# A gated mix of a 2D spectral filter and a state-space recurrence on one core: the last recurrence units moved ahead of the last output tiles, and the start reordered

## The chip, the cores and the metric

The kernel runs on one core of one Trainium2 chip. The core has five engines, each with its own instruction stream taken in order: PE multiplies matrices (its weight loads are listed apart as PEld), DVE, ACT and POOL work elementwise, SP only issues transfers (DMAs), which ACT and POOL can issue too. PE writes its products into PSUM, from which ACT or DVE copies them to SBUF, the working memory. The metric is the device time of one execution in microseconds (us), the median of several.

## What is computed

The input x has 2048 rows (time) of 1024 features. Branch A filters x in the frequency plane, branch B runs a complex linear recurrence with 1024 states over time, and a gate per row mixes the two.

```python
X = rfft2(x); a = irfft2(X * (w_r + 1j * w_i)).astype(bfloat16)        # branch A
Lam_bar = exp(exp(log_dt) * Lam); Bu = einsum("bld,pd->blp", x, B_bar)  # branch B
for t in range(L): h = Lam_bar * h + Bu[:, t]
y = 2 * einsum("blp,dp->bld", hseq, Cmat).real + x * Dskip
g = sigmoid((x * gate_w).sum(-1, keepdims=True))
return g * a + (1 - g) * y
```

## The kernel before

Transforms and the products of branch B are matrix products on PE. The order of PE, DVE and ACT is written out by hand: within these three engines the instructions stand in the order in which the Python code emits them. SP and POOL are ordered by the framework's own scheduler. The work runs in these stages:

- **Fronts.** x arrives in eight loads of 512 KB (`load_x`, L192). `turn_x(j)` (L625) transposes one of 16 row groups on PE and copies it to `xQ` on ACT; `fold(j)` (L631) makes `preT` of it on DVE. A front j (L730) turns two row groups, folds one, takes one step of the transform along the features (`ps_fd` L330 on PE, `X` L333 on ACT) and one of the transform along time (`ps_s` L344 to L347 on PE, `A` L349 on DVE for j under 7, else on ACT), and stores `A` to DRAM. From j = 8 each front also has half a recurrence unit and pieces of the rotation tables (`make_tab`, L203: DVE makes the angle `ang`, ACT `rot_kk`, `sn_f`, `cs_f` and the scaled copies `t`, DVE the table `tab`). After fronts 9, 11, 13 and 15 `gate` (L656) makes four columns of the gate; its result `zsb` goes through DRAM on POOL's queue (L664, L666) and comes back as `zt`.
- **Recurrence units.** `unit(c, q)` (L247) is a chunk c of 256 rows and a half q of the states. PE makes the two halves `psu` (L295, 32 products each), ACT copies each to `h` (L297), and DVE then has seven pieces of work: two rotations back (L256, L257), a join (L262 to L265), two scans (L269), the carry (L275 to L277), two rotations forth (L281, L282) and a join (L287, L288). The pieces wait in a Python list; `vector(us)` (L306) emits as many as an assumed budget allows, and `vector_until(c)` all that chunk c needs.
- **Spectral middle.** After the fronts, "w", "z", "q" and "qn" correct one column (through DRAM and back as `Bcol`, L357 and L360, on POOL's queue, and with `gate_end`, L668, which makes `omg`, `gB` and `grat` from `zt`). Then 16 groups are multiplied by the filter (L445 to L482) and 8 turned back (L487 to L501), each interleaved with a half unit or half of an `early` tile.
- **Output tiles** of 128 rows. The first ten are `early(tb)` (L566): branch B alone is finished, scaled by `omg` and parked in DRAM as `ye`. `late_tile(i)` (L605) closes one later: `spectral` (L582: eight products `ps_id` L588, a copy L591 on ACT, four additions L593 to L597 on DVE), plus the parked tile (L607 on DVE), then the store. The last six, `own_tile(tb)` (L610), hold both branches in one PSUM tile: 16 products L557 and five small ones per half (L561 with `dgD`, the diagonal of the skip weights; L564 adds the spectral part `ga`), a copy L618 on ACT, the store. `own` (L857) makes `ga` of the next tile between the two halves.

The last stage runs from the end of chunk 6's first unit: `unit(6, 1)`, own tile 10, `unit(7, 0)`, own tile 11, `unit(7, 1)`, then own tiles 12 to 15 with the ten late tiles beside them; the counts in the table of L868 say how many late tiles follow each half.

Of the kernel before, what the change touches and what calls it, by code (L numbers as in the profile page):

```python
# [13 lines left out]
FP32 = mybir.dt.float32  # L14
# [91 lines left out]
def kernel(  # L106
# [215 lines left out]
    def gfnet():  # L322
# [16 lines left out]
        for j in range(16):  # L339
            X1 = X1_next  # L340
            if j + 1 < 16:
                X1_next = fd(j + 1)
            psa = psA.tile([P, 2, K], FP32, name="ps_s1", tag="ps")
            nc.tensor.matmul(psa[:, 0, :], lhsT=T3_sb[:, j, 0, :], rhs=X1[:, 0, :], start=True, stop=False)  # L344
            nc.tensor.matmul(psa[:, 0, :], lhsT=T3_sb[:, j, 1, :], rhs=X1[:, 1, :], start=False, stop=True)
            nc.tensor.matmul(psa[:, 1, :], lhsT=T3_sb[:, j, 0, :], rhs=X1[:, 1, :], start=True, stop=False)
            nc.tensor.matmul(psa[:, 1, :], lhsT=T3_sb[:, j, 2, :], rhs=X1[:, 0, :], start=False, stop=True)  # L347
            A1 = gta.tile([P, 2, K], BF16, name="A1", bufs=3)
            (nc.vector.tensor_copy if j < 7 else nc.scalar.copy)(out=A1, in_=psa)  # L349
            if j:  # L350
                nc.vector.tensor_copy(out=Acol[:, j - 1, :], in_=A1s[j - 1][:, :, 0])
            A1s[j] = A1
            nc.sync.dma_start(out=turn1_dram[j].rearrange("r m k -> m r k"), in_=A1)
            yield "s1"
# [148 lines left out]
    def after_ia():  # L503
        ictx.close()
        hpool[1] = ctx.enter_context(tc.tile_pool(name="hpB", bufs=NHB, side="right", reuse_waits="tile"))
        lp = ctx.enter_context(tc.tile_pool(name="lp", bufs=1, side="right", reuse_waits="tile"))
        fft["lp"] = lp
        load_xs(0)
        fft["dgD"] = lp.tile([P, 8, P], BF16, name="dgD")
        for d8 in range(8):  # L510
            nc.vector.tensor_scalar_mul(out=fft["dgD"][:, d8, :], in0=ident, scalar1=dskT[:, d8:d8 + 1])
        fft["gt"] = bctx.enter_context(tc.tile_pool(name="gt", bufs=3, side="right", reuse_waits="tile"))
        fft["wp"] = bctx.enter_context(tc.tile_pool(name="wp", bufs=1, side="right", reuse_waits="tile"))
        fft["Sel"] = fft["gt"].tile([P, 4, P], BF16, name="Sel_sb", tag="gc1", bufs=2)
        nc.sync.dma_start(out=fft["Sel"], in_=cKRS.rearrange("p (i m) -> p i m", m=P)[:, 2:6])
        fft["Wb"] = [fft["wp"].tile([P, 2, 2, K], BF16, name=f"Wb{i}") for i in range(3)]
        for w in fft["Wb"]:
            nc.gpsimd.memset(w[:, 0, :, 0:1], 1.0)
            nc.gpsimd.memset(w[:, 1, :, 0:1], 0.0)
# [111 lines left out]
    def fold(j):  # L631
        preTs[j] = gta.tile([P, 8, P], BF16, name="preT", bufs=4)
        nc.vector.tensor_add(out=preTs[j][:, 0:4], in0=xQ[:, 0:4, j, :], in1=xQ[:, 4:8, j, :])
        nc.vector.tensor_sub(out=preTs[j][:, 4:8], in0=xQ[:, 0:4, j, :], in1=xQ[:, 4:8, j, :])

    load_x(0)
    nc.sync.dma_start(out=fft["G"], in_=cG)
    load_x(1)
    load_T3(0, 4)
    for i in range(2, 5):  # L640
# [5 lines left out]
    for j in range(2):  # L646
        turn_x(j)
        fold(j)

    turn_x(2)  # L650
    fold(2)
    assert step() == "fd"
    zsb = cpool.tile([P, 16], FP32, name="zsb")
    zt = cpool.tile([P, 16], FP32, name="zt")

    def gate(r0, n):  # L656
        zps = psX.tile([P, n], FP32, name="zps_g", tag="pt")
        for r in range(r0, r0 + n):
            for d8 in range(8):
                nc.tensor.matmul(zps[:, r - r0:r - r0 + 1], lhsT=xQ[:, d8, r, :], rhs=gwT[:, d8:d8 + 1],  # L660
                                 start=(d8 == 0), stop=(d8 == 7))
        nc.vector.tensor_copy(out=zsb[:, r0:r0 + n], in_=zps)
        if r0 + n == 16:
            nc.gpsimd.dma_start(out=z_dram, in_=zsb)  # L664
            with nc.allow_non_contiguous_dma(reason="gate by token tiles"):
                nc.gpsimd.dma_start(out=zt, in_=z_dram.rearrange("(t a) j -> (a j) t", a=8))  # L666
# [63 lines left out]
    def front(pieces=0):  # L730
        j = at[0]
        at[0] += 1
        for r in (2 * j + 3, 2 * j + 4):
            if r < 16:
                turn_x(r)
        if 3 <= j + 2 < 16:
            fold(j + 2)
        assert step() == "s1"
        for load, *args in order.get(j, ()):
            load(*args)  # L740
        for _ in range(pieces):
            next(tables, None)
# [65 lines left out]
    tables = chain(*(make_tab(jp) for jp in range(4)))  # L808
    while at[0] < 16:
        j = at[0]  # L810
        front(0 if j < 4 else 1 if j < 6 else 2 if j < 9 else 3)
        if j >= 8:
            halves(ssm, 1)
        if j >= 9:
# [13 lines left out]
    for v, n in (("w", 3), ("z", 2), ("q", 2), ("qn", 1), ("s2", 0), ("uv", 1)):  # L828
        assert step() == v
        if v == "z":  # L830
            gate_end()
        for _ in range(n):
            halves(ssm, 1)
            vector(3.0)
    for g in range(16):
        assert step() == "is1"
        assert step() == "uv"
# [23 lines left out]
            yield v  # L861

    ga[NEARLY] = spectral(NEARLY, grat, own_home(NEARLY))
    for _ in chain(unit(6, 1), own(10), unit(7, 0), own(11), unit(7, 1)):
        vector(4.0)
    for i in range(4):
        yl[i] = late_load(i)
    for tb, counts in ((12, (0, 2)), (13, (1, 1)), (14, (2, 2)), (15, (2, 0))):  # L868
        for _, n in zip(own(tb), counts):
            vector(4.0)  # L870
            for _ in range(n):
# [35 lines left out]
```

## Time and profile before

| what | us |
|---|---|
| median of 3 runs (lowest to highest) | 371.21 (369.28 to 371.55) |
| the profiled execution's own time | 370.46 |
| span, from its first to its last instruction | 367.9 |
| PE busy, 92% of the span | 338.0 |
| DVE busy, 81% | 298.1 |
| ACT busy, 48% | 177.1 |
| transfers: 62.17 MB, mean 169 GB/s | |

Numbers of the trace are us from the span's start. A row of the timeline has the start, the busy time, the engine, the line in the code, the operation, what is written and read, the count of merged instructions, and in brackets how long the engine was idle before and what released it. PE's products overlap, so 32 products of 273 ns each pass in about 3.5 us; distances between starts are the safer measure. The profile's clock row shows what the throttle granted (0.989 on average).

### The profile page before, as it was taken

What the parts mean: (1) busy time and instruction counts of PE and PEld (TensorE: products, weight loads), DVE (VectorE), ACT (ScalarE), POOL (GpSimd) and SP (SyncE); (2) the same over time, 40 slices, a digit from 0 to 9 for tenths busy, and PEclk for the clock granted to TensorE, in tenths of its full rate; (3) what the DMA queues carried; (4) which work ended last, traced back from release to release, by engine and by line L of the source; (5) the groups of instructions that cost most, each with busy time, mean ns of one, the idle gap of its engine ahead of it and who ended that gap; (6) DMA issues with size and microseconds to landing.
All of it is one profiled execution on the core that took longest, in us unless ns stands there. A gap on an engine that the chain in (4) does not pass through costs nothing.

```text
span 367.9 us, 6395 instructions
## 1 busy us (share of the span) xinstructions
PE 338.0 (92%) x2488; PEld 226.6 (62%) x2521; DVE 298.1 (81%) x483; ACT 177.1 (48%) x216; POOL 21.0 (6%) x54
## 2 busy tenths in 40 slices
PE   2899899599999999999999999999999999999980
PEld 1455367376876665666656576795957667565540
DVE  1168855889779999999999999929368699999596
ACT  3499987465431265555656325453432223253620
POOL 7310111100030000000000000000000000000000
PEclk9999999999999999999999999999999999999995
DMA  7999999975582148899997367551202262025863
GB/s 225 331 316 202 208 232 205 208 204 132 182 208 22 67 132 199 237 252 274 265 275 199 108 177 206 141 172 57 87 12 76 57 228 59 2 57 163 238 228 115
DMA packets 83310, 62.17 MB, mean 169 GB/s; under 512 B 54320, under 2 KB 71248, under 8 KB 83024
## 3 DMA queue, kind: packets, MB, share of 16 engines
q1 hardware_dynamic: 82688, 61.70, 62.4%
q0 software_dynamic: 512, 0.05, 1.1%
q8 instruction: 19, 0.31, 0.4%
q14 instruction: 11, 0.09, 0.1%
q10 hardware_dynamic: 80, 0.01, 0.0%
HBM read 31.32 MB, written 17.84 MB: 134 GB/s over the span
## 4 chain that ended last, share of the span: by engine, by line
PE 65%; DVE 17%; DMA 9%; issue 4%; ACT 4%; SPq 0%; ACTq 0%; DVEq 0%
PE ps_y L557 22%; PE psu L295 21%; PE ps_fd L330 4%; PE ps_is L497 4%; DVE h L269 3%; DMA turn_scratch<-A 3%; DMA CT<-in_A_x_dram 2%; PE ps_id L588 2%; PE ps_is L472 2%; PE ps_is L473 2%; PE ps_s L448 2%; PE ps_y L561 2%; DMA out_dram<-raw 1%; DMA raw<-turn_scratch 1%; DMA turn_scratch<-C 1%
## 5 line engine op out<-in xcount | busy, mean ns | idle before, releaser
L295 PE MATMUL psu<-xQ,BT 128*128 128x256 bf16 x1024 | 116.1, 273 | 3.9 <-ACT h L297 3.3
L557 PE MATMUL ps_y<-CT,h 128*128 128x512 bf16 x493 | 113.5, 379 | 0.9
L295 PEld LDWEIGHTS <-BT 128*128 128x128 bf16 x1024 | 100.1, 98 | 19.9 <-issue 4.9
L557 PEld LDWEIGHTS <-h 128*128 128x128 bf16 x512 | 50.3, 99 | 55.0
L269 DVE TENSOR_TENSOR_SCAN h<-rz,h 128x1024 bf16<-128x1024 f32 x32 | 72.3, 2281 | 0.3
L297 ACT CAST h<-psu 128x1024 bf16<-128x1024 f32 x32 | 32.3, 1010 | 59.9 <-PE psu L295 59.9
L330 PE MATMUL ps_fd<-G_sb,preT 128*128 128x512 bf16 x118 | 30.9, 396 | 4.0 <-ACT X L333 1.8
L256 DVE TENSOR_TENSOR su<-h,tab 128x2048 bf16<-128x2048 bf16 x16 | 19.6, 1222 | 17.8 <-ACT h L297 17.3
L575 ACT ACTIVATE ye<-ps_y,omg 128x512 f32<-128x512 f32 x20 | 12.7, 683 | 36.6 <-PE ps_y L561 25.2
L333 ACT CAST X<-ps_fd 128x1024 bf16<-128x1024 f32 x16 | 20.9, 1307 | 7.4 <-PE ps_fd L330 6.6
L330 PEld LDWEIGHTS <-preT 128*128 128x128 bf16 x128 | 12.3, 100 | 17.4 <-issue 4.4
L499 ACT CAST ZT<-ps_is 128x1024 bf16<-128x1024 f32 x16 | 15.4, 1020 | 10.7 <-PE ps_is L497 10.7
L257 DVE TENSOR_TENSOR h<-h,tab 128x2048 bf16<-128x2048 bf16 x16 | 19.6, 1225 | 1.0
L282 DVE TENSOR_TENSOR h<-h,tab 128x2048 bf16<-128x2048 bf16 x16 | 19.6, 1225 | 0.5
L281 DVE TENSOR_TENSOR sg<-h,tab 128x2048 bf16<-128x2048 bf16 x16 | 19.5, 1219 | 0.1
L450 ACT CAST X<-ps_s 128x1024 bf16<-128x1024 f32 x16 | 16.2, 1014 | 6.8 <-PE ps_s L448 6.8
L628 PE MATMUL pt<-ident,CT 128*128 128x128 bf16 x128 | 10.3, 240 | 8.5 <-DMA CT<-in_A_x_dram 8.5
L629 ACT COPY xQ<-pt 128x1024 bf16<-128x1024 bf16 x16 | 15.5, 1016 | 5.4 <-PE pt L628 5.4
L475 ACT CAST C<-ps_is 128x1024 bf16<-128x1024 f32 x16 | 16.1, 1007 | 2.9 <-PE ps_is L473 2.8
L588 PE MATMUL ps_id<-raw,ZT 128*128 128x256 bf16 x128 | 15.8, 273 | 0.4 <-ACT raw L591 0.4
L591 ACT ACTIVATE raw<-ps_id,grat 128x1024 bf16<-128x1024 f32 x6 | 6.7, 1114 | 18.3 <-PE ps_id L588 18.3
L497 PE MATMUL ps_is<-KRS_sb,raw 128*128 128x128 bf16 x128 | 15.3, 311 | 0.2 <-DMA raw<-turn_scratch 0.2
(182 smaller groups left out, 386.9 us busy)
## 6 DMA issues: line engine op xcount, KB each, us to landing
y_scratch<-ye SPq DMA_DIRECT2D x20, 256.0 KB, 3.9
BT<-y_scratch SPq DMA_DIRECT2D x10, 512.0 KB, 5.0
CT<-in_A_x_dram SPq DMA_DIRECT2D x8, 512.0 KB, 10.3
turn_scratch<-A SPq DMA_DIRECT2D x16, 256.0 KB, 3.1
Bb<-turn_scratch SPq DMA_DIRECT2D x16, 256.0 KB, 4.7
turn_scratch<-C SPq DMA_DIRECT2D x16, 256.0 KB, 3.9
raw<-turn_scratch SPq DMA_DIRECT2D x16, 256.0 KB, 4.4
Wb<-in_A_w_r_dram SPq DMA_DIRECT2D x32, 127.8 KB, 3.7
```

Of the source, the lines that this page charges most:

```text
L256: nc.vector.tensor_mul(out=su, in0=u[:, ::-1], in1=bc(1))
L257: nc.vector.tensor_mul(out=u, in0=u, in1=bc(0))
L269: nc.vector.tensor_tensor_scan(out=seg, data0=rz[:, js].rearrange("p j t -> p (j t)"), data1=seg, initial=0.0, op0=ALU.mult, op1=ALU.add)
L281: nc.vector.tensor_mul(out=sg, in0=u[:, ::-1], in1=bc(3))
L282: nc.vector.tensor_mul(out=u, in0=u, in1=bc(2))
L295: nc.tensor.matmul(psu[:, j, :], lhsT=BT[4 * q + j][:, ri, d8, :], rhs=xQ[:, d8, :, 16 * c:16 * (c + 1)], start=(d8 == 0), stop=(d8 == 7))
L297: nc.scalar.copy(out=u[:, ri].rearrange("p b (q j) -> p b q j", j=16), in_=psu.rearrange("p b (j q) -> p b q j", j=16))
L330: nc.tensor.matmul(ps[:, cls, :], lhsT=preTs[j][:, 4 * cls + d4, :], rhs=G_sb[:, cls, d4, :], start=(d4 == 0), stop=(d4 == 3))
L333: nc.scalar.copy(out=X1.rearrange("p r (i c) -> p c r i", c=2), in_=ps.rearrange("p c (r i) -> p c r i", r=2))
L497: nc.tensor.matmul(pv[:, :, g::4], lhsT=Cq[:, g, P * kc:P * (kc + 1)], rhs=KRS_sb[:, 1, :], start=True, stop=True)
L557: nc.tensor.matmul(psy[:, 512 * dh:512 * (dh + 1)], lhsT=hs[c, jb // 4][:, ri, jb % 4, P * tq:P * (tq + 1)], rhs=CT[ri][:, jb, 512 * dh:51 ...
L588: nc.tensor.matmul(pse[:, slot, :], lhsT=ZT_t[:, i, tb, :], rhs=fft["Gi"][:, i, :], start=(kb == 0), stop=(kb == 1))
```

## The change

Six edits, in the order of the program:

- **Start.** Eight throwaway products (zeros times zeros, into a PSUM tile that nothing reads) stand on PE ahead of everything, four more after the first two row groups are turned. The table `G` is loaded in two halves. The first feature transform stands ahead of the third row group's turn.
- **Folds** are made one front earlier: `fold(j + 3)` in front j.
- **Copies.** `A` is copied by DVE up to j = 9 instead of 6; `zsb` by ACT instead of DVE. Front 9 emits two table pieces instead of three.
- **`dgD`** (eight small scalings on DVE) leaves the spot right after the fronts and is emitted between two pieces of unit (1, 0) in stage "w".
- **POOL's queue**: not in the diff, but its four small transfers come out in another order.
- **End.** Units (6, 1), (7, 0) and (7, 1) come one after another ahead of own tile 10; the late tiles follow the halves of own tiles 11 to 14 one by one, the last two the first half of own tile 15.

```diff
-            (nc.vector.tensor_copy if j < 7 else nc.scalar.copy)(out=A1, in_=psa)
+            (nc.vector.tensor_copy if j < 10 else nc.scalar.copy)(out=A1, in_=psa)
...
-        for d8 in range(8):
-            nc.vector.tensor_scalar_mul(out=fft["dgD"][:, d8, :], in0=ident, scalar1=dskT[:, d8:d8 + 1])
...
+    idle = gta.tile([P, K], BF16, name="idle", tag="A1", bufs=3)
+    nc.vector.memset(idle, 0.0)
+
+    def keep_warm(n):
+        psw = psA.tile([P, 2, K], FP32, name="psw", tag="ps")
+        for i in range(n):
+            nc.tensor.matmul(psw[:, i % 2, :], lhsT=idle[:, 0:P], rhs=idle, start=True, stop=True)
+
+    keep_warm(8)
     load_x(0)
-    nc.sync.dma_start(out=fft["G"], in_=cG)
+    for cls in range(2):
+        nc.sync.dma_start(out=fft["G"][:, cls], in_=cG[:, cls])
...
     for j in range(2):
         turn_x(j)
         fold(j)
-
+    keep_warm(4)
+
+    assert step() == "fd"
     turn_x(2)
     fold(2)
-    assert step() == "fd"
...
-        nc.vector.tensor_copy(out=zsb[:, r0:r0 + n], in_=zps)
+        nc.scalar.copy(out=zsb[:, r0:r0 + n], in_=zps)
...
-        if 3 <= j + 2 < 16:
-            fold(j + 2)
+        if 3 <= j + 3 < 16:
+            fold(j + 3)
...
-        front(0 if j < 4 else 1 if j < 6 else 2 if j < 9 else 3)
+        front(0 if j < 4 else 1 if j < 6 else 2 if j < 10 else 3)
...
-        for _ in range(n):
+        for i in range(n):
             halves(ssm, 1)
             vector(3.0)
+            if v == "w" and i == 1:
+                for d8 in range(8):
+                    nc.vector.tensor_scalar_mul(out=fft["dgD"][:, d8, :], in0=ident, scalar1=dskT[:, d8:d8 + 1])
...
-    for _ in chain(unit(6, 1), own(10), unit(7, 0), own(11), unit(7, 1)):
+    for _ in chain(unit(6, 1), unit(7, 0), unit(7, 1)):
         vector(4.0)
     for i in range(4):
         yl[i] = late_load(i)
-    for tb, counts in ((12, (0, 2)), (13, (1, 1)), (14, (2, 2)), (15, (2, 0))):
+    for tb, counts in ((10, (0, 0)), (11, (1, 1)), (12, (1, 1)), (13, (1, 1)), (14, (1, 1)), (15, (2, 0))):
```

What the edits do to the engines' order shows at three places. The first is ACT in fronts 10 to 12, before: the copies `X` (L333) and `A` (L349) of a front, the table work (`rot_kk`, `sn_f`, `cs_f`, `t`), and `h` (L297), which empties the only PSUM tile that the recurrence units have in this stage.

```order
L333 CAST X_848<-ps_fd 128x2x512
L349 CAST A_855<-ps_s_850 128x1024
L224 ACTIVATE t_759<-cs_f,ci 128x256 x2
L771 ACTIVATE rot_kk<-ang 128x512
L772 ACTIVATE sn_f<-ang 128x512
L297 CAST h<-psu 128x1024
L333 CAST X_931<-ps_fd 128x2x512
```

The same engine after, from the same front 10 on (lines past L633 have moved by some nine: L780 is L771, L781 is L772, L783 is L774):

```order
L333 CAST X_862<-ps_fd 128x2x512
L349 CAST A_869<-ps_s_864 128x1024
L783 ACTIVATE cs_f<-rot_kk,chpi 128x512
L219 ACTIVATE t_878<-sn_f,ci 128x256 x2
L224 ACTIVATE t_879<-cs_f,ci 128x256 x2
L297 CAST h<-psu 128x1024
L333 CAST X_949<-ps_fd 128x2x512
```

Before, `rot_kk` of the fourth table, which needs DVE's `ang`, stands between front 10's `A` and the copy `h`; after, the third table's rest stands there, and the fourth `rot_kk` comes a front later, behind front 11's `A`.

The second place is the end of POOL's queue, after its last presets of a filter tile: the small transfers of the gate (`zsb` out, `zt` back) and of the one column (`Acol` out, `Bcol` back). Before:

```order
L518 MEMSET Wb_1403 128x2
L519 MEMSET Wb_1403 128x2
L664 DMA z_scratch<-zsb 128x16
L357 DMA col_scratch<-Acol 128x32
L666 DMA zt<-z_scratch 128x16x1
L360 DMA Bcol<-col_scratch 128x16x2
```

After (L673 is L664, L675 is L666):

```order
L516 MEMSET Wb_1412 128x2
L517 MEMSET Wb_1412 128x2
L357 DMA col_scratch<-Acol 128x32
L360 DMA Bcol<-col_scratch 128x16x2
L673 DMA z_scratch<-zsb 128x16
L675 DMA zt<-z_scratch 128x16x1
```

The gate's way out and back stood around the column's; it now stands wholly behind it.

The third place is ACT at the end, which copies for PE and so shows PE's order: `h` is a unit, `raw` (L591) the spectral part of an own tile, `BT` (L591) that of a late tile, L618 the close of an own tile. Before, from the spectral part of own tile 10 on:

```order
L591 ACTIVATE raw<-ps_id,grat 128x1024
L297 CAST h<-psu 128x1024 x2
L591 ACTIVATE raw<-ps_id,grat 128x1024
L618 ACTIVATE raw<-ps_y,omg 128x1024
L297 CAST h<-psu 128x1024 x2
L591 ACTIVATE raw<-ps_id,grat 128x1024
L618 ACTIVATE raw<-ps_y,omg 128x1024
L297 CAST h<-psu 128x1024 x2
L591 ACTIVATE raw<-ps_id,grat 128x1024
L618 ACTIVATE raw<-ps_y,omg 128x1024
L591 ACTIVATE BT_131<-ps_id,gB 128x1024
L591 ACTIVATE BT_132<-ps_id,gB 128x1024
```

After, from the same place (L589 is L591, L616 is L618):

```order
L589 ACTIVATE raw<-ps_id,grat 128x1024
L297 CAST h<-psu 128x1024 x6
L589 ACTIVATE raw<-ps_id,grat 128x1024
L616 ACTIVATE raw<-ps_y,omg 128x1024
L589 ACTIVATE raw<-ps_id,grat 128x1024
L589 ACTIVATE BT_131<-ps_id,gB 128x1024
L616 ACTIVATE raw<-ps_y,omg 128x1024
L589 ACTIVATE BT_132<-ps_id,gB 128x1024
L589 ACTIVATE raw<-ps_id,grat 128x1024
L589 ACTIVATE BT_133<-ps_id,gB 128x1024
L616 ACTIVATE raw<-ps_y,omg 128x1024
L589 ACTIVATE BT_134<-ps_id,gB 128x1024
```

The six copies of three units now stand together ahead of every own tile, and the first late tile follows one own tile instead of three, one per half from there.

On DVE the end follows suit: the pieces of units (6, 1), (7, 0) and (7, 1) come first, with the spectral parts of own tiles 11 to 13 and late tiles 0 to 2 among them; seven late tiles and the parts of own tiles 14 and 15 stand behind.

## The prediction

> **What bounds the kernel now.** I read the busy time by stages first, then the timeline of the stages that look odd, and in them what ended PE's and DVE's idle times.
>
> ```profile
> 60.00:97.00 37.00, 31.91 (x284) 23.20 (x287) 34.46 (x58) 20.53 (x25) 2.26 (x8) 1.00 0.71 170
> 97.00:131.60 34.60, 33.82 (x307) 24.21 (x307) 28.64 (x69) 8.26 (x10) 3.43 (x4) 1.00 0.45 117
> 131.60:241.00 109.40, 108.63 (x733) 71.41 (x744) 106.91 (x130) 58.76 (x80) 0.00 (x0) 1.00 0.80 213
> 275.50:357.00 81.50, 80.72 (x557) 53.11 (x563) 70.65 (x105) 27.41 (x26) 0.00 (x0) 1.00 0.39 120
> 357.00:367.90 10.90, 0.00 (x0) 0.00 (x0) 7.60 (x14) 2.12 (x2) 0.00 (x0) 0.65 0.38 145
> ```
>
> The stage rows give, after the length, busy time of PE, PEld, DVE, ACT and POOL. PE is the bound wherever it has anything to do: from 131.6 on it stands still under 1% of the time until 357. What isn't PE's work is at three places: the start, some 5 us between 60 and 97, and the last 10.9 us, in which PE does nothing and DVE is busy for 7.6. In the last stage DVE has 70.65 + 7.60 = 78.3 us of work in 92.4, so it ends late because it idles early. The change touches all three places.
>
> **Start.** The waits of PE and the third load of x:
>
> ```profile
> 4.36 1.89 PE L628 MATMUL pt<-ident,CT 128*128 128x128 bf16 x16 [4.36 <-DMA CT<-in_A_x_dram]
> 10.35 1.03 PE L628 MATMUL pt<-ident,CT 128*128 128x128 bf16 x8 [4.10 <-DMA CT<-in_A_x_dram]
> 11.38 3.41 PE ps_fd L330 x8
> 14.95 1.29 PE L628 MATMUL pt<-ident,CT 128*128 128x128 bf16 x16
> 19.72 1.90 PE ps_fd L330 x8
> ...
> 4.33 0.33 SPq L193 DMA_DIRECT2D CT<-in_A_x_dram  x1
> ...
> DMA to landing us min/median/max: 10.3/10.3/10.3
> ...
> L629 ACT COPY xQ<-pt 128x1024 bf16<-128x1024 bf16 x16 | 15.5, 1016 | 5.4 <-PE pt L628 5.4
> ```
>
> PE ran at half rate until about 15 us: eight products of `ps_fd` took 3.41 us there (from the chain) and 1.90 later. After the change the first transform runs ahead of the second load and, warmed by the throwaway products, at nearly the full rate: done by some 9 us instead of 14.8. But front 0 also turns a row group of the third load, which lands at 4.33 + 10.3 = 14.6, 0.3 us ahead of the row at 14.95: PE's queue stops there again. Of front 0's 1.29 us of turns one half, 0.65, is done while it waits; with 0.3 less of lag the gain is 0.9, and ACT, which takes 1.0 for each turned row group and so is as loaded as PE in these fronts, passes on 0.6. The eight throwaway products take 3.41 at the half rate and end, from about 1.1 on, at 4.5: 0.15 after the first load, hidden under the third. The zeroed tile costs DVE one small preset, in the idle time before its first fold. Splitting `G` adds one issue on SP (0.33 for its neighbours), ahead of loads whose time is the queue's, not the issue's. Both ends: the transfers' order changes, so the third load may come 2 us earlier (gain 3); or PE may fall back to the half rate in the wait before it (then 1.7 lost, below). I take **-0.6**.
>
> The Trainium skill, TensorE: Matmul & The Clock Gate, Part 1: The HAM clock gate, says that PE's clock halves after an idle window of about 3.4 us and doubles after as much work. The rows agree on the size (3.41 against 1.90). By that rule the last wait here, about 12.4 to 14.6, is 2.2 us and too short; the sum would stay -0.6. That the rule speaks of a free-running window, with no product in it, is what could make it otherwise.
>
> **Fronts 10 to 13.** Two of PE's waits:
>
> ```profile
> 51.47 0.92 DVE L225 SCALAR_TENSOR_TENSOR tab<-cs_f,cr,t 128x256 bf16<-128x256 f32 x2 [4.16 <-ACT t L219]
> 65.74 1.68 PE L330 MATMUL ps_fd<-G_sb,preT 128*128 128x512 bf16 x7 [1.63 <-DVE preT L633]
> 69.42 0.63 ACT L771 ACTIVATE rot_kk<-ang 128x512 f32<-128x512 f32 x1 [6.64 <-DVE ang L769]
> 70.47 0.99 ACT L297 CAST h<-psu 128x1024 bf16<-128x1024 f32 x1
> 71.52 3.65 PE L295 MATMUL psu<-xQ,BT 128*128 128x256 bf16 x32 [3.01 <-ACT h L297]
> 73.44 0.74 ACT L774 ACTIVATE cs_f<-rot_kk,chpi 128x512 f32<-128x512 f32 x1
> 75.66 1.00 ACT L297 CAST h<-psu 128x1024 bf16<-128x1024 f32 x1
> 78.40 3.66 PE L295 MATMUL psu<-xQ,BT 128*128 128x256 bf16 x32
> ```
>
> The first wait, 1.63, is for a fold that stood behind a scan; folded a front earlier, it is there. The second, 3.01, is the copy `h` standing on ACT behind `rot_kk`, which waited 6.64 us for DVE's `ang`, behind that scan too. After the change the copy stands behind the third table's work, whose `ang` is long made: the unit half of front 10 is through at 64.0, its copy at 65.2, the transform of front 11 at 65.8, its second step at 66.7, and the half that began at 71.52 begins there, 4.8 earlier. It ends at 70.2, and now ITS copy stands behind the whole fourth table: `ang` at about 69.7, then 1.05 (69.42 to 70.47) and 2.22 (73.44 to 75.66) of table work, so the copy ends at 74.1 and the next half, at 78.40 before, starts then. What is late next is this copy, with a wait of about 1.1, and the gain is 4.2.
>
> Three `A` copies more on DVE are 3 x 1.2 us; DVE's idle 4.16 before 51.47 takes them, and ACT is relieved of three of 1.0. `zsb`, four tiny copies, goes to ACT, which is busy for 20.5 of 37 us here.
>
> **The column and the gate.**
>
> ```profile
> 101.05 0.56 POOL L664 DMA_DIRECT2D z_scratch<-zsb  x1 [24.42 <-DVE Acol L356]
> 103.38 1.39 DVE L511 TENSOR_SCALAR dgD<-ident,vecF 128x128 bf16<-128x128 bf16 x8 [2.55 <-DMA turn_scratch<-A]
> 111.85 0.21 ACT L670 ACTIVATE g_bf<-zt 128x16 bf16<-128x16 f32 x1 [1.48 <-DMA zt<-z_scratch]
> 118.10 1.27 ACT L575 ACTIVATE ye<-ps_y,omg 128x512 f32<-128x512 f32 x2 [6.04 <-DVE omg L674]
> 119.97 3.65 PE L295 MATMUL psu<-xQ,BT 128*128 128x256 bf16 x32
> ...
> z_scratch<-zsb POOLq DMA_DIRECT2D x1, 8.0 KB, 5.3
> col_scratch<-Acol POOLq DMA_DIRECT2D x1, 8.0 KB, 4.9
> zt<-z_scratch POOLq DMA_DIRECT2D x1, 8.0 KB, 5.2
> ```
>
> `dgD` made DVE wait 2.55 for a store; moved behind two scans of unit (1, 0) its 1.39 ends at about 107, just before the first early tile wants it (107.3, four early). That keeps DVE in step with PE's 4.2: some 4.0. But POOL now sends the gate behind the whole round trip of the column. From `Acol`, at about 96: 4.9, the issue of `Bcol` 1.2, 5.3, 5.2 and gaps of 0.5 make 113.1 for `zt`; then ACT's `g_bf`, which blocks ACT's queue, DVE's `omg` behind `gB` on DVE's queue, and `ye` until 115.2. The PSUM tile that it frees is wanted by the unit half of the row at 119.97, minus 4.2 to 4.5: 115.5. So PE's wait is hidden with 0.3 to spare; four transfers of 5 us beside a 1.5 MB load are not that exact, and I count 0.5. Bounds: no gain (0) and all of it (4.6). Net of fronts and gate: **-3.7**. Until 275 PE and DVE then keep their order and move forward together.
>
> **End.**
>
> ```profile
> 275.50 7.15 PE L295 MATMUL psu<-xQ,BT 128*128 128x256 bf16 x64 [0.53 <-ACT ye L575]
> 287.25 3.62 PE L557 MATMUL ps_y<-CT,h 128*128 128x512 bf16 x16
> ...
> 291.14 7.15 PE L295 MATMUL psu<-xQ,BT 128*128 128x256 bf16 x64
> ...
> 283.75 0.68 DVE L288 TENSOR_TENSOR h<-h,sg 128x1024 bf16<-128x1024 bf16 x1
> 288.59 0.42 DVE L593 TENSOR_TENSOR raw<-raw 128x512 bf16<-128x512 bf16 x1 [4.16 <-ACT raw L591]
> 290.07 1.22 DVE L256 TENSOR_TENSOR su<-h,tab 128x2048 bf16<-128x2048 bf16 x1
> 302.91 1.23 DVE L256 TENSOR_TENSOR su<-h,tab 128x2048 bf16<-128x2048 bf16 x1
> 346.83 0.42 DVE L593 TENSOR_TENSOR raw<-raw 128x512 bf16<-128x512 bf16 x1 [3.61 <-DMA out_dram<-raw]
> 348.38 0.42 DVE L593 TENSOR_TENSOR BT<-BT 128x512 bf16<-128x512 bf16 x1
> 351.10 0.42 DVE L593 TENSOR_TENSOR BT<-BT 128x512 bf16<-128x512 bf16 x1
> 363.58 1.23 DVE L607 TENSOR_TENSOR BT<-BT,BT 128x1024 bf16<-128x1024 f32 x1
> ```
>
> In the old clock: PE runs the three units 275.5 to 296.5 (7.0 each), then halves of own tiles of 3.87 (287.25 to 291.14) and spectral parts of 0.87. Four own tiles, four parts and six late tiles put own tile 14 at 296.5 + 31.0 + 8.7 = 336.2, the end at 356.5. DVE goes on at 284.4 without the 4.16: unit (6, 1) takes 12.84 (290.07 to 302.91), the other two, without a carry, 12.5; a late tile 2.72 (348.38 to 351.10), an own part 1.5. Unit (6, 1) ends at 297.2; unit (7, 0) with two parts, and 1.4 of waiting for the first, at 314.1; unit (7, 1) with three late tiles and a part at 336.3. Own tile 14 needs it: PE waits some 0.1. Seven late tiles and two parts more end at 358.4. The last store took from 364.8 to the span's end, 3.1; so 361.5 against 367.9: **-6.4**. The 3.61 at 346.83 goes as well, since each own part stands longer after the store that it overwrites. Bounds: PE's own end with copy and store, 360.6 (gain 7.3); if both idle times stay, 7.8 lost, none.
>
> **Sum.** 0.6 + 3.7 + 6.4 = 10.7: a span of 357.2, and 370.46 - 10.7 = 359.8 for the profiled execution, which lies 0.75 under the median of the runs. I don't correct for that.
>
> **Rivals.**
> - *Only the end gains.* The fronts trade one waiting copy for another (after the change the whole fourth table stands ahead of one `h`), and PE's 4.64 come back. For it: ACT had two such waits. Against it: DVE makes `ang` at about the same time as before, and the copy before it goes free. 359.8 + 3.7 = 363.5. Chance 0.13.
> - *PE at the half rate at front 0* (its turns and transform at 3.41 instead of 1.72): 1.7 lost in place of 0.6 gained, 362.1. The wait of 4.10 before 10.35 was followed by the half rate, but so was the work before it. Chance 0.15.
> - *PE waits for unit (7, 1).* It is due within 0.1 us of PE; each wait of DVE before it moves both the last two own tiles and the seven late tiles. With a second such idle time (3.61) the end comes at 363.4. Chance 0.12.
> - *Slower: the gate.* ACT, DVE and PE all end up behind `zt`. It decides only if `zt` lands 16 us later than I have it (then PE's half starts at 131 and eats 11 us and 1% more): the four transfers would have to take twice their rows. Chance 0.03, 375 or more.
>
> **How the numbers follow.** The forecast has 0.57, with a range of its own of 356.5 (the third load early) to 362; the four rivals the rest. The range 356.5 to 364.5 takes in the first three and leaves out the last and combinations of them, about 0.15. About 1%, 3.7 us, is what a measurement can tell from no change: all cases but the last, and a few combinations, stay under 367.5. Faster 0.92, within 1% 0.05, slower 0.03.
>
> **What would show it.** PE at front 0 still waiting for x at about 14.6, then products at 0.22 us distance; no wait of PE for `preT`, one of about 1 us for `h`, and the first half of unit (1, 0) some 4 us earlier; `zt` behind `Bcol`, with ACT idle before `g_bf` and PE not; DVE without a gap over 1.5 us in the last stage, its last addition 2 us after PE's last product. I am wrong if PE's last product comes later than 353, or DVE's last addition more than 5 us behind it.

## The result, and the profile after

| | kernel before | changed kernel |
|---|---|---|
| median of the runs, us | 370.91 (369.28 to 371.55, 4 runs) | 360.27 (359.84 to 360.60, 4 runs) |
| the profiled execution's own time | 370.46 | 360.31 |
| span | 367.9 | 358.4 |

The ratio of the times is 0.9719, with a 95% interval of 0.9685 to 0.9753. The forecast was 359.8, the chance of faster by over 1% was 0.92. The sum came out within half a microsecond; two of its three terms did not, and this part is about them.

In three later sets of runs, beside which the experiments were timed, the kernel before had medians of 371.62, 371.80 and 371.93. So the experiments are compared by their ratio to the kernel before, and, more finely, by stages of their profiled executions. All waits of PE in the changed kernel above 0.2 us, from the timeline (start, busy time, engine, line, operation, and in brackets how long PE stood still and what released it):

```profile
1.22 3.59 PE L640 MATMUL psw<-idle 128*128 128x512 bf16 x8 [1.22 <-DVE idle L635]
11.22 0.62 PE L626 MATMUL pt<-ident,CT 128*128 128x128 bf16 x8 [1.65 <-DMA CT<-in_A_x_dram]
12.94 0.61 PE L626 MATMUL pt<-ident,CT 128*128 128x128 bf16 x8 [0.89 <-ACT xQ L627]
15.49 1.04 PE L626 MATMUL pt<-ident,CT 128*128 128x128 bf16 x8 [1.95 <-DMA CT<-in_A_x_dram]
16.75 3.19 PE L330 MATMUL ps_fd<-G_sb,preT 128*128 128x512 bf16 x7 [0.22 <-issue]
29.89 1.89 PE L330 MATMUL ps_fd<-G_sb,preT 128*128 128x512 bf16 x8 [0.59 <-ACT X L333]
43.53 1.89 PE L330 MATMUL ps_fd<-G_sb,preT 128*128 128x512 bf16 x8 [0.58 <-ACT X L333]
46.88 1.89 PE L330 MATMUL ps_fd<-G_sb,preT 128*128 128x512 bf16 x8 [0.60 <-ACT X L333]
56.27 3.65 PE L295 MATMUL psu<-xQ,BT 128*128 128x256 bf16 x32 [0.55 <-ACT h L297]
76.58 3.65 PE L295 MATMUL psu<-xQ,BT 128*128 128x256 bf16 x32 [0.30 <-ACT zsb L671]
94.30 3.65 PE L295 MATMUL psu<-xQ,BT 128*128 128x256 bf16 x32 [0.24 <-ACT h L297]
...
272.33 17.84 PE L295 MATMUL psu<-xQ,BT 128*128 128x256 bf16 x162 [0.53 <-ACT ye L573]
```

The waits of 1.63 for `preT` and 3.01 for `h` are gone, and so is that of 0.59 for `Bcol`. The start has become worse: the third load of x lets PE go at 15.49 (14.95 before, as the prediction shows), and then eight turns take 1.04 and seven products of `ps_fd` 3.19, at half rate.

Three of these rows serve as marks, since every kernel here has them: the transform step at 46.88, the last unit half beside the fronts at 94.30, and the first half of unit (6, 1) at 272.33. The same in the kernel before (the third, 275.50, stands in the prediction):

```profile
44.66 1.89 PE L330 MATMUL ps_fd<-G_sb,preT 128*128 128x512 bf16 x8 [0.60 <-ACT X L333]
...
96.12 3.65 PE L295 MATMUL psu<-xQ,BT 128*128 128x256 bf16 x32 [0.24 <-ACT h L297]
```

The distances between the marks, worked out from such rows of each kernel's profiled execution (us). "Ratio" is the time of the runs over that of the kernel before; the marks are of one execution each.

| kernel | ratio to before | to mark 1 | mark 1 to 2 (fronts) | 2 to 3 (gate, spectral middle) | 3 to the end |
|---|---|---|---|---|---|
| before | 1 | 44.66 | 51.46 | 179.38 | 92.40 |
| changed | 0.9719 | 46.88 | 47.42 | 178.03 | 86.07 |
| a_oldstart | 0.9658 | 44.46 | 47.78 | 179.03 | 86.13 |
| a_g1 | 0.9712 | 45.16 | 49.78 | 178.43 | 86.13 |
| a_fill | 0.9826 | 49.55 | 49.03 | 178.03 | 86.09 |
| a_nowarm | 0.9728 | 46.42 | 49.58 | 178.03 | 86.07 |
| b_end | 0.9830 | 44.50 | 51.42 | 180.17 | 86.11 |
| a_fold2 | 0.9749 | 45.01 | 51.44 | 178.03 | 86.02 |
| a_tab | 0.9907 | 45.88 | 57.01 | 178.03 | 85.98 |
| a_A7 | 0.9660 | 46.42 | 46.88 | 178.03 | 86.07 |
| a_old_A7 | 0.9649 | 44.64 | 47.79 | 178.08 | 87.19 |
| a_fill_pool | 0.9605 | 43.76 | 47.42 | 178.03 | 86.19 |
| a_dgd | 0.9713 | 46.38 | 48.48 | 178.02 | 86.02 |
| a_zsb | 0.9741 | 46.03 | 47.85 | 179.12 | 86.10 |

So the span's 9.5 us are made of +2.2 at the start, -4.0 in the fronts, -1.35 from there to unit (6, 1), and -6.3 at the end. The first two are no fixed sizes. The kernels that keep the edits of the start and undo another one (a_fold2, a_tab, a_A7, a_dgd, a_zsb) have mark 1 anywhere between 45.01 and 46.42, so the start cost 0.4 to 2.2 us in one execution or another, and those with an early mark 1 mostly give it back by mark 2.

The end is as it was to be. The last product of PE in the kernel before, and then the last of PE and the last additions of DVE in the changed kernel:

```profile
356.60 0.38 PE L564 MATMUL ps_y<-raw,ident 128*128 128x512 bf16 x1
...
352.88 0.38 PE L562 MATMUL ps_y<-raw,ident 128*128 128x512 bf16 x1
353.58 0.42 DVE L595 TENSOR_TENSOR BT<-BT 128x512 bf16<-128x512 bf16 x1
354.03 1.22 DVE L605 TENSOR_TENSOR BT<-BT,BT 128x1024 bf16<-128x1024 f32 x1
```

DVE ends 2.0 us behind PE (355.25 against 353.26), where it ended 7.8 behind it before (its last addition there, from 363.58 on, stands in the prediction). In the stage rows of the changed kernel (length, then busy time of PE, PEld, DVE, ACT and POOL), from mark 3 to PE's end and from there on, DVE's work now lies beside PE's:

```profile
272.30:353.30 81.00, 80.56 (x557) 53.11 (x563) 76.25 (x116) 28.35 (x28) 0.00 (x0) 1.00 0.42 131
353.30:358.40 5.10, 0.00 (x0) 0.00 (x0) 1.92 (x3) 1.11 (x1) 0.00 (x0) 1.00 0.41 154
```

### The profile page after: what moved, and what is told of

It reads as the page before. It is cut to its first block, busy times and chain, and to the rows that moved or that the text cites. A ratio compares the mean times of both kernels' runs of the same rounds, so it can differ in the third digit from the quotient of the medians.

```text
span 358.4 us, 6423 instructions
## 1 busy us (share of the span) xinstructions
PE 342.0 (95%) x2500; PEld 228.2 (64%) x2533; DVE 302.0 (84%) x483; ACT 174.8 (49%) x217; POOL 21.4 (6%) x54
## 4 chain that ended last, share of the span: by engine, by line
PE 82%; ACT 5%; DVE 5%; DMA 4%; issue 3%; ACTq 0%; DVEq 0%
PE ps_y L555 29%; PE psu L295 28%; PE ps_fd L330 5%; PE ps_is L497 4%; PE ps_id L586 3%; DMA CT<-in_A_x_dram 3%; PE ps_is L472 2%; PE ps_is L473 2%; PE ps_y L559 2%; ACT X L333 2%; PE ps_s L448 2%; DMA vec<-in_B_Lambda_im_dram 1%; PE pt L626 1%; ACT h L297 1%; DVE h L269 1%
## 5 line engine op out<-in xcount | busy, mean ns | idle before, releaser
L297 ACT CAST h<-psu 128x1024 bf16<-128x1024 f32 x32 | 32.3, 1010 | 60.1 <-PE psu L295 60.1
L333 ACT CAST X<-ps_fd 128x1024 bf16<-128x1024 f32 x16 | 20.9, 1305 | 9.1 <-PE ps_fd L330 7.6
L349 DVE CAST A<-ps_s 128x1024 bf16<-128x1024 f32 x10 | 12.2, 1222 | 10.4 <-PE ps_s L347 9.5
L631 DVE TENSOR_TENSOR preT<-xQ 128x512 bf16<-128x512 bf16 x16 | 7.0, 439 | 11.1 <-ACT xQ L627 11.1
L589 ACT ACTIVATE raw<-ps_id,grat 128x1024 bf16<-128x1024 f32 x6 | 6.7, 1114 | 18.1 <-PE ps_id L586 18.1
```

Source lines behind the costliest of these rows:

```text
L297: nc.scalar.copy(out=u[:, ri].rearrange("p b (q j) -> p b q j", j=16), in_=psu.rearrange("p b (j q) -> p b q j", j=16))
L333: nc.scalar.copy(out=X1.rearrange("p r (i c) -> p c r i", c=2), in_=ps.rearrange("p c (r i) -> p c r i", r=2))
```

## The experiments

Names that begin with a are the changed kernel with an edit, b is the kernel before with one. The first four take the start apart.

**a_oldstart: the start of before.**

```diff
-    keep_warm(8)
...
-    for cls in range(2):
-        nc.sync.dma_start(out=fft["G"][:, cls], in_=cG[:, cls])
+    nc.sync.dma_start(out=fft["G"], in_=cG)
...
-    keep_warm(4)
-    assert step() == "fd"
     turn_x(2)
     fold(2)
+    assert step() == "fd"
```

> The changed kernel with the start of the kernel before (no throwaway products, G in one load, the first transform behind the third row group). Theory: the new start lost 2.2 us (the step of front 7's transform begins at 46.88 instead of 44.66) and everything behind it only moves with it, so this ends at 360.3 - 2.2 = 358.1. Rival: what comes behind is held by something else too (the column's round trip, DVE's units), which eats what the start gives: 359.5 or more.

358.85 us (357.98 to 359.61), ratio 0.9658 (0.9621 to 0.9695). Mark 1 is back at 44.46, mark 2 comes 2.1 earlier than in the changed kernel. The theory holds in size. One microsecond of it is given back later in the profiled execution: PE waits 0.72 for a load `raw` at 216.02, and the distance from mark 2 to 3 is 179.03. So the new start, taken as a whole, costs about 2 us; the ratios give 2.3, with intervals that overlap.

**a_g1: `G` in one load**, with the rest of the new start.

```diff
-    for cls in range(2):
-        nc.sync.dma_start(out=fft["G"][:, cls], in_=cG[:, cls])
+    nc.sync.dma_start(out=fft["G"], in_=cG)
```

> The changed kernel with the table G in one load. Theory: the second half of G took a place in the queue, so that SP issued the third load of x at 5.61 instead of 4.33; with one load it lands near 14.6 instead of 15.4, and the end comes 0.9 earlier, at 359.4, with the clock at front 0 still halved. Rival: the third load is bound by what the transfers move, not by its issue: it lands at 15.4 as before, and the time stays at 360.3.

360.73 us (359.83 to 362.01), ratio 0.9712 (0.9673 to 0.9750): no change that can be measured. The third load of x is the first of the three in this row of SP's queue, in the changed kernel and then in a_g1 (start, time that SP spends on the issues):

```profile
5.61 2.10 SPq L193 DMA_DIRECT2D CT<-in_A_x_dram  x3
```

```profile
4.49 2.44 SPq L193 DMA_DIRECT2D CT<-in_A_x_dram  x3
```

With `G` in one piece the third load is issued 1.1 us sooner, PE goes on at 14.85 instead of 15.49, and mark 1 comes 1.7 sooner. That the split is the cause isn't shown. In the other profiled executions with `G` in two pieces the issue comes between 4.63 (a_nowarm) and 5.78 (a_A7), and PE, where it waits for the load, goes on between 14.52 (a_fold2) and 15.34 (a_A7). With `G` in one piece and the old start (a_oldstart) the issue comes at 4.48, and PE waits for that load until 15.57. So the split does put the issue off, but when the load lands doesn't follow the issue; the rival is as good as the theory here.

Another part of the 1.7 us is the clock. The stage rows have the granted clock in the third place from the end; a_g1:

```profile
14.00:17.50 3.50, 2.43 (x12) 1.56 (x14) 0.76 (x2) 1.58 (x2) 1.78 (x9) 0.55 1.03 408
17.50:21.00 3.50, 3.50 (x29) 2.01 (x28) 1.46 (x4) 2.35 (x3) 1.92 (x11) 0.96 1.04 414
```

If the clock is either 1.00 or 0.50, it was at half for 3.4 us here. In the changed kernel it was for 6.8 (rows under the next run), and its seven products take 3.19 instead of 2.51. At mark 2 a_g1 is 0.6 later than the changed kernel. Something between the two marks took the gain back; what, the next run shows.

**a_fill: 14 more throwaway products**, so that PE doesn't stand still while x arrives.

```diff
     assert step() == "fd"
+    keep_warm(6)
     turn_x(2)
...
         for r in (2 * j + 3, 2 * j + 4):
+            if r == 4:
+                keep_warm(8)
             if r < 16:
                 turn_x(r)
```

> The changed kernel with 14 throwaway products more: six ahead of the third row group, eight ahead of the fifth, in PE's waits for the second and third load. Theory: the clock fell at 13.8 because PE stood still in patches (1.65, 0.89 and 1.95 us); kept busy it stays full, seven products of front 0 take 1.67 instead of 3.19 and the step behind them 0.4 less: 1.9 less, 358.4. Rival: the clock falls at 13.8 all the same, or the products stand in the way of the turns: 360.3 to 361.

364.99 us (364.36 to 365.90), ratio 0.9826 (0.9785 to 0.9867): 4 us slower, though what the theory says of the clock is right. The granted clock in the changed kernel:

```profile
12.00:14.00 2.00, 0.65 (x10) 0.50 (x8) 0.95 (x4) 0.99 (x2) 0.00 (x0) 0.95 0.94 358
14.00:16.00 2.00, 0.51 (x5) 0.51 (x6) 0.97 (x5) 1.22 (x3) 0.36 (x2) 0.50 1.02 401
...
18.00:20.00 2.00, 2.00 (x6) 0.76 (x5) 0.00 (x0) 0.02 (x1) 1.49 (x9) 0.50 1.03 411
20.00:22.00 2.00, 2.00 (x21) 1.32 (x20) 0.76 (x1) 1.59 (x2) 0.00 (x0) 0.85 1.06 425
```

In a_fill it is 1.00 in every such row from 10 to 24, and front 0's step takes 1.89 for eight products. But then, from its timeline, DVE and PE:

```profile
36.46 1.22 DVE L349 CAST A<-ps_s 128x1024 bf16<-128x1024 f32 x1 [4.43 <-DMA turn_scratch<-A]
...
47.11 1.23 DVE L349 CAST A<-ps_s 128x1024 bf16<-128x1024 f32 x1 [3.64 <-DMA turn_scratch<-A]
```

```profile
37.74 0.38 PE L344 MATMUL ps_s<-X,raw 128*128 128x512 bf16 x1 [2.03 <-DVE A L349]
...
39.36 3.25 PE L330 MATMUL ps_fd<-G_sb,preT 128*128 128x512 bf16 x8
...
48.39 0.38 PE L344 MATMUL ps_s<-X,raw 128*128 128x512 bf16 x1 [2.45 <-DVE A L349]
...
49.55 3.06 PE L330 MATMUL ps_fd<-G_sb,preT 128*128 128x512 bf16 x7
```

The clock falls again, behind each of these two waits: the eight products take 3.25 and the seven 3.06, where the full rate gives 1.89 and 1.67. The clock line of its page, in 40 slices of 9.1 us, shows it in the fifth and sixth:

```profile
PEclk9999889999999999999999999999999999999999
```

So the account closes: the step of front 1 starts 3.0 us earlier than in the changed kernel (18.89 against 21.93), PE then waits 4.7 for `A` and loses 2.8 by the clock, and mark 2 is 4.3 us late. Most of that is lost by mark 1, which is the row at 49.55.

`A` has three buffers. A copy into one waits until the store of three fronts ago has read it, and PE's next step waits for the copy. The stores stand in SP's queue, and there, from the same kernel:

```profile
14.86 4.98 SPq L200 DMA_TRANSPOSE BT<-in_B_B_re_dram  x1
19.89 4.41 SPq L200 DMA_TRANSPOSE BT<-in_B_B_im_dram  x1
24.35 1.31 SPq L200 DMA_TRANSPOSE BT<-in_B_B_re_dram  x1
25.77 0.51 SPq L353 DMA_DIRECT2D turn_scratch<-A  x1
```

The transposing loads of B hold SP for 1.3 us each and more, and the first store of `A` has three of them ahead of it here. In the changed kernel it has one, in the kernel before none: its first store is issued at 20.12, ahead of the first such load at 20.55. No line of the diff says so: SP's order is the scheduler's, and it came out another way in each of the three. In all, DVE waits 10.8 us for stores of `A` in a_fill, 0.9 in the changed kernel.

**a_fill_pool: the same, with the first ten stores of `A` issued by POOL.**

```diff
-            nc.sync.dma_start(out=turn1_dram[j].rearrange("r m k -> m r k"), in_=A1)
+            (nc.gpsimd if j < 10 else nc.sync).dma_start(out=turn1_dram[j].rearrange("r m k -> m r k"), in_=A1)
```

> The kernel with 14 more throwaway products, and its first ten stores of A issued by POOL instead of SP. Theory: its front 1 was 3 us early, but the stores of A stood in SP's queue behind transposing loads of 1.31 us each, and DVE stood for them 4.43, 1.37 and 3.64 us; on POOL's queue they go at once, PE's waits for A (2.03, 0.18, 2.45) go, and the time falls from 365.0 to 357 to 359. Rival: the stores are slow because the transfers are saturated, whoever issues them: 364 to 365.

357.15 us (356.92 to 357.51), ratio 0.9605 (0.9576 to 0.9635): 7.8 us faster than a_fill, and the fastest of all that ran. The stores leave as soon as the copy is done, and DVE waits for PE, not for a store:

```profile
19.65 0.76 POOL L353 DMA_DIRECT2D turn_scratch<-A  x1 [0.16 <-DVE ang L792]
23.14 0.74 POOL L353 DMA_DIRECT2D turn_scratch<-A  x1 [2.73 <-DVE A L349]
26.62 0.72 POOL L353 DMA_DIRECT2D turn_scratch<-A  x1 [2.75 <-DVE sTC L798]
```

```profile
39.87 1.22 DVE L349 CAST A<-ps_s 128x1024 bf16<-128x1024 f32 x1 [0.67 <-PE ps_s L347]
43.19 1.23 DVE L349 CAST A<-ps_s 128x1024 bf16<-128x1024 f32 x1 [0.21 <-PE ps_s L347]
```

The rival, that transfers are slow whoever issues them, falls: the bytes are the same. The same waits took back a_g1's gain, and a_nowarm's below: PE waits for `A` 1.94 at 48.98 in the one, 1.40 and 1.65 at 45.56 and 49.96 in the other, and DVE's copies there wait 2.21 and 2.34, and 3.41 and 1.65, for a store. What stores on POOL would give without the 14 products isn't shown.

**a_nowarm: no throwaway products.**

```diff
-    keep_warm(8)
...
-    keep_warm(4)
```

> The changed kernel without any throwaway products. Theory: the first transform then runs at half rate, 3.5 us instead of 2.06, and ends near 11, still ahead of the second load at 11.2; the clock is at half in front 0 either way. So they are worth nothing as they stand: 360.3, at most 0.5 more. Rival: without them front 0 and 1 are at the half rate for longer: 361.8.

361.56 us (360.61 to 361.84), ratio 0.9728 (0.9687 to 0.9768), the same as with them as far as can be measured. The first transform takes 3.60 from 6.90 and ends ahead of the second load, as the theory has it. The throwaway products of the change buy nothing, because what they speed up waits for the second load anyway, and because they stop before the waits in which the clock falls.

The next four take apart the fronts and the end.

**b_end: the kernel before with the new end.**

```diff
-    for _ in chain(unit(6, 1), own(10), unit(7, 0), own(11), unit(7, 1)):
+    for _ in chain(unit(6, 1), unit(7, 0), unit(7, 1)):
...
-    for tb, counts in ((12, (0, 2)), (13, (1, 1)), (14, (2, 2)), (15, (2, 0))):
+    for tb, counts in ((10, (0, 0)), (11, (1, 1)), (12, (1, 1)), (13, (1, 1)), (14, (1, 1)), (15, (2, 0))):
```

> The kernel before with the new order of the end alone (three units together, own tiles 10 to 15 behind them, late tiles one by one). Theory: the end's gain needs nothing of the other edits: 6.3 us off, 364.6, with PE's last product near 356.5 in the old clock and DVE's last addition 2 us behind it. Rival: the gain hangs on the fronts' lead, without which DVE comes to the units later: half of it, 368.

365.63 us (364.05 to 366.58), ratio 0.9830 (0.9791 to 0.9868), 6.2 us off 371.8. PE's last product starts at 356.64, DVE's last addition ends at 359.02, and the stage takes 86.11 instead of 92.40. The gain at the end stands by itself.

**a_fold2: folds two fronts ahead.**

```diff
-        if 3 <= j + 3 < 16:
-            fold(j + 3)
+        if 3 <= j + 2 < 16:
+            fold(j + 2)
```

> The changed kernel with the folds two fronts ahead again instead of three. Theory: PE waits again for preT in front 11, some 1.6 us: 361.9. Rival: the wait came from the table work ahead of it on DVE, which has moved, so that the fold is there in time either way: 360.3.

362.51 us (362.04 to 362.74), ratio 0.9749 (0.9714 to 0.9784). PE waits 1.71 for `preT` again, at 68.97, and mark 2 is 2.15 later than in the changed kernel, at 96.45. The theory holds by the trace; the ratios alone, 1.1 us apart with intervals that overlap, would not show it. (That the stretch between marks 1 and 2 is 4.0 longer is not all the fold: mark 1 came 1.9 earlier, and waits of 0.52 and 1.79 for `A` took that back.)

**a_tab: three table pieces in front 9.**

```diff
-        front(0 if j < 4 else 1 if j < 6 else 2 if j < 10 else 3)
+        front(0 if j < 4 else 1 if j < 6 else 2 if j < 9 else 3)
```

> The changed kernel with three table pieces in front 9 again instead of two. Theory: this one number put ACT's rot_kk of the fourth table behind the copy h; with three pieces rot_kk waits for DVE's ang ahead of that copy, and PE's wait of 3.0 us for h comes back: 363. Rival: the earlier folds and the copies moved to DVE removed that wait, and the number is worth under 0.5: 360.3 to 360.8.

368.46 us (367.35 to 369.07), ratio 0.9907 (0.9872 to 0.9941): most of the change's gain is gone. ACT, then PE, in its timeline, and two of its stage rows:

```profile
73.85 0.63 ACT L780 ACTIVATE rot_kk<-ang 128x512 f32<-128x512 f32 x1 [7.31 <-DVE ang L778]
...
75.95 5.99 PE L295 MATMUL psu<-xQ,BT 128*128 128x256 bf16 x32 [5.89 <-ACT h L297]
```

```profile
72.00:76.00 4.00, 0.05 (x1) 0.05 (x1) 3.93 (x7) 2.15 (x4) 0.94 (x1) 0.74 1.14 228
76.00:80.00 4.00, 4.00 (x20) 2.75 (x20) 2.10 (x7) 4.00 (x7) 1.12 (x4) 0.50 0.51 156
```

The copy `h` stands behind `rot_kk` again, now for 5.89 us, and that is long enough for the clock to fall: the 32 products that follow take 5.99 instead of 3.65. The wait and the 2.34 by the clock make 8.2 of the 8.6 us by which mark 2 is late. The theory holds, and its price was too low.

**a_A7: `A` copied by ACT from j = 7 on.**

```diff
-            (nc.vector.tensor_copy if j < 10 else nc.scalar.copy)(out=A1, in_=psa)
+            (nc.vector.tensor_copy if j < 7 else nc.scalar.copy)(out=A1, in_=psa)
```

> The changed kernel with A copied by DVE up to j = 6 again, by ACT from 7. Theory: three copies of 1.0 us come back onto ACT ahead of h; PE's wait for h near 56.3 grows from 0.55 by about 1: 361.3. Rival: ACT has idle time ahead of its rot_kk in these fronts (3.97 and 2.16), which takes the copies: 360.3.

359.14 us (358.83 to 359.54), ratio 0.9660 (0.9631 to 0.9689). The theory fails: undoing the edit doesn't cost 1 us. If anything the edit itself costs, in the stretch between marks 1 and 2 by 0.5 us. One row of the changed kernel's DVE, and its ACT:

```profile
46.97 1.23 DVE L349 CAST A<-ps_s 128x1024 bf16<-128x1024 f32 x1 [0.87 <-DMA turn_scratch<-A]
...
50.80 0.63 ACT L780 ACTIVATE rot_kk<-ang 128x512 f32<-128x512 f32 x1 [3.97 <-DVE ang L778]
...
59.58 0.63 ACT L780 ACTIVATE rot_kk<-ang 128x512 f32<-128x512 f32 x1 [2.16 <-DVE ang L778]
```

and that of a_A7:

```profile
48.63 0.63 ACT L780 ACTIVATE rot_kk<-ang 128x512 f32<-128x512 f32 x1
...
57.26 0.63 ACT L780 ACTIVATE rot_kk<-ang 128x512 f32<-128x512 f32 x1
```

On DVE the copies stand ahead of `ang`, and the one at 46.97 waits for a store besides. So ACT gets the angle 2.2 us later (1.7, counted from mark 1), and the rest of its table work and `h` come behind it. PE's waits of 0.55 and 0.30 fit that, the second for the `h` that ends just ahead of the `zsb` in its row; a_A7 has neither, but waits 0.48 for an `A`. The place of the copies is not the whole cause, though: a_fill_pool has them on DVE too, but no wait for a store, and there the first of the two waits is gone, while the second is 0.95. The difference of the ratios would be 2.2 us, with intervals that just overlap; the profiled executions show 0.5 in this stretch and 0.5 by mark 1, and nothing elsewhere. How much of it is the edit and how much one execution against another stays open.

**a_old_A7: both undone.** The edits of a_oldstart and of a_A7 together.

> The changed kernel with two of its edits undone together: the start of the kernel before, and A copied by ACT from j = 7 on. Theory: the start's loss (ratio 0.9719 to 0.9658) and the copies' loss (0.9719 to 0.9660) lie at different places, the first ahead of 20 us, the second at 44 to 77, and add up: a ratio near 0.960, 356.5 against a kernel before of 371.4. Rival: both give the same wait back (PE standing for A's store in fronts 7 and 8), so that the second adds under 0.5 us: 0.965, 358.4.

359.05 us (357.99 to 359.67), ratio 0.9649 (0.9617 to 0.9681). The rival holds: beside a_oldstart (0.9658) the second adds nothing that can be measured; between marks 1 and 2 both take 47.8. With the old start PE still waits 0.44 for an `A` and 0.79 for an `h`, on ACT now, since ACT's copy stands for the store in the place of DVE's. Its last stage is 1.1 longer than the others' in the profiled execution, all of it in the last store, which takes 4.2 instead of 3.1.

**a_dgd and a_zsb** put back one small thing each.

```diff
+        for d8 in range(8):
+            nc.vector.tensor_scalar_mul(out=fft["dgD"][:, d8, :], in0=ident, scalar1=dskT[:, d8:d8 + 1])
...
-            if v == "w" and i == 1:
-                for d8 in range(8):
-                    nc.vector.tensor_scalar_mul(out=fft["dgD"][:, d8, :], in0=ident, scalar1=dskT[:, d8:d8 + 1])
```

> The changed kernel with the eight scalings of dgD back at their old place, right behind the fronts. Theory: DVE waits there for the store of an A again, some 2.5 us, and hands on part of it to the early tiles and the gate: 361.3 (1.0 more). Rival: DVE has the slack, and nothing comes out of it: 360.3.

361.29 us (360.79 to 361.68), ratio 0.9713 (0.9686 to 0.9740): worth nothing. From mark 2 to 3 it takes 178.02, as the changed kernel. DVE does not even wait at the old place any more: the last store of `A` is issued at 95.75 and is done when DVE comes to `dgD` at 99.38. In the kernel before it was issued at 97.01 and landed past 103. Why it took so much longer there stays open.

```diff
-        nc.scalar.copy(out=zsb[:, r0:r0 + n], in_=zps)
+        nc.vector.tensor_copy(out=zsb[:, r0:r0 + n], in_=zps)
```

> The changed kernel with zsb copied by DVE again; its four small transfers then stand on POOL in the old order, the gate's around the column's. Theory: Bcol is issued an issue later (1.2 us) and PE waits for it by 0.6 to 0.8 as in the kernel before: 361.0. Rival: the gate comes back earlier in exchange and gives as much: 360.3.

362.15 us (361.05 to 363.01), ratio 0.9741 (0.9710 to 0.9772). The distance from mark 2 to 3 is 179.12 instead of 178.03. This edit alone turns POOL's queue round. POOL and PE in a_zsb:

```profile
98.85 0.56 POOL L673 DMA_DIRECT2D z_scratch<-zsb  x1 [16.55 <-DVE Wc_f L391]
99.40 0.55 POOL L357 DMA_DIRECT2D col_scratch<-Acol  x1
104.49 1.19 POOL L675 DMA_DIRECT2D zt<-z_scratch  x1 [4.54 <-DMA z_scratch<-zsb]
105.67 1.16 POOL L360 DMA_DIRECT2D Bcol<-col_scratch  x1
```

```profile
110.39 0.17 PE L405 MATMUL zps<-Bcol,K_sb 128*128 128x16 bf16 x1 [0.93 <-DMA Bcol<-col_scratch]
```

PE's wait for `Bcol` is back, with 0.93; in the changed kernel `Bcol` is issued at 104.69 and PE doesn't wait. The theory's step holds, at 1.1 us in this stretch; the ratios alone can't tell this kernel from the changed one.

## Why the prediction was right, and where it wasn't

- **End, -6.4.** Measured -6.3, in the changed kernel and in b_end alone. The steps are in the trace: DVE without a gap over 1.1 us from 275 on, its last addition 2.0 us after PE's last product, the last store 3.1 from there to the span's end. That PE's units and tiles take as long in either order, and that DVE ends late because it idles early, was the whole of it. The sign set for being wrong, PE's last product later than 353, stayed away by a hair: it starts at 352.88, because this stage begins 1.1 later than forecast (272.33 against 275.5 - 4.3).
- **Fronts, -4.2.** Measured -4.0 between marks 1 and 2. The two waits went for the reasons given: the fold a front earlier (a_fold2), and `h` no longer behind the fourth table's `rot_kk` (a_tab). The step "its copy stands behind the whole fourth table", with a wait of 1.1, was too dear by 0.8: PE waits 0.30 there. In its place PE waits 0.55 at 56.27, which was not in the sum. The step that missed it is "Three `A` copies more on DVE are 3 x 1.2 us; DVE's idle 4.16 before 51.47 takes them". That idle time lay ahead of `tab`, behind `ang`; the copies stand ahead of `ang`, for which ACT waits (a_A7), and one of them waits for a store (0.87). An idle time takes only work that stands at its place in the queue. The sign "the first half of unit (1, 0) some 4 us earlier" failed by the start: it comes 1.8 earlier (76.58 against 78.40).
- **Column and gate, 0.5 lost.** Measured 1.35 gained. `zt` lands at 113.8 against 113.1, but that is luck: the column left at 99.21 instead of about 96, and the chain from there took 14.6 instead of 17.1. As forecast, ACT stands for it (5.29) and PE not at all. What failed is that only one side of the turned queue was priced. The column came forward, and PE's 0.59 for `Bcol` went; a_zsb gives 1.1 for the turn alone. In all PE stands still for 0.85 less between marks 2 and 3 (1.38 instead of 2.23). The other 0.5 of the 1.35 lies in PE's busy time (176.65 instead of 177.15), and its cause stays open. The move of `dgD`, a part of this term, is worth nothing (a_dgd).
- **Start, -0.6.** Measured +2.2 in the profiled execution, and about 2 by a_oldstart. The step that failed is that PE keeps the full rate which the throwaway products gave it. The products did warm it (2.06 for the first transform), but the clock fell at 13.8, in the wait for the third load. By then PE had stood still for 1.65 and 0.89 us and for the first 0.3 of that wait, never longer. The Trainium skill (TensorE: Matmul & The Clock Gate, Part 1: The HAM clock gate) has it fall after an idle window of about 3.4 us. In the 3.4 us from 10.4 to 13.8 PE was busy for 1.44, so the measurement decides against a window that must be empty, and against "By that rule the last wait here, about 12.4 to 14.6, is 2.2 us and too short". The rival that has PE at half rate at front 0 came true; it had 1.7 for it. With the waits filled the clock stayed (a_fill), so the cause is shown. The step on `G`, "ahead of loads whose time is the queue's, not the issue's", is not shown to have failed: the issue came 1.3 later (5.61 instead of 4.33), but the landings of the other executions don't follow the issue (a_g1). And one thing isn't in the prediction at all: the transposing load that SP now takes ahead of the first store of `A`. In the changed kernel it costs little, because the start is late anyway; as soon as the start is mended it costs most of what was mended (a_g1, a_nowarm) or more (a_fill).

The sum was right by luck: the start was forecast 2.8 too good and the column 1.9 too bad. The trace's span is 1.2 longer than the sum's, and the execution has 0.7 less around it. Only the end, and in the main the fronts, were forecast for reasons that hold.

The experiments lead to a version that beats both: a_fill_pool, at 0.9605. The start then costs nothing (mark 1 at 43.76, 0.9 ahead of the kernel before), and the rest of the change is untouched.

## What to carry to other kernels

When a transfer's issue is free, look at what stands behind it on the same queue: here a store for which PE never waited in the kernel before stood behind transposing loads, held a buffer, then a copy, then PE, and turned gains at the start into a wait some 20 us later. The order of a queue that a scheduler writes must be compared before and after like one written by hand, on both sides of whatever changes places. Throwaway products are worth their place only across the waits in which the clock would fall, not ahead of them.

## What the runs showed of the hardware

- In the changed kernel the granted clock fell to 0.50 at 13.8 and came back at about 20.6, 6.8 us later, though PE was busy without a pause from 16.75 on. Fourteen products in the waits kept it at 1.00 there. It differs from one execution to the next. With the new start and without those products it fell in all eight kernels, between about 12.2 (a_zsb) and 15.0 (a_nowarm), for 3.4 us in three (a_g1, a_fold2, a_nowarm) and for 6.8 in five, if it is either 1.00 or 0.50 in the stage rows.
- The length of one wait didn't decide it: a wait of 3.01 us in the kernel before, at 71.52, left the clock at 1.00, and in a_fill waits of 2.03 and 2.45 were followed by a fall.
- A wait of 5.89 us in the middle of the kernel cost 2.34 us more by the clock (5.99 for 32 products that else take 3.65).
- A transposing load of B holds SP for 1.3 us or more per issue, up to 6.9 at the start (a_fill_pool), beside the loads of x; a plain store of `A` mostly holds it for 0.4 to 0.5. On POOL the same store takes 0.73, and PE waited for no `A` there.
- At the start of the kernel before, the record shows a granted clock of 1.00 while eight products of `ps_fd` take 3.41 instead of 1.90: there the products' own times show the rate, and the clock doesn't. Its stage row:

```profile
10.00:12.00 2.00, 1.65 (x10) 1.13 (x11) 0.00 (x0) 0.58 (x1) 0.90 (x2) 1.00 1.05 131
```
